# One core, a Fourier transform and two feed-forward layers: the start-up's loads, folds and conversions put in another order

## The chip, the core and the metric

The kernel runs on one core of a Trainium2 chip. The metric is device time in microseconds (us) of one execution; the time before is the median of three runs. Everything else here is read from one execution that was profiled: TensorE (PE) multiplies matrices, PEld is its loading of weights; VectorE (DVE), ScalarE (ACT) and GpSimd (POOL) work elementwise; SyncE (SP) issues the transfers. Each engine works through its own list in order.

## What is computed

```python
X = np.fft.fft(np.fft.fft(x, axis=1), axis=2).real      # x: 2 x 3008 x 256
h = X.reshape(6016, 256) @ moe_w_in                     # 256 x 2048
y = (h * (1 / (1 + np.exp(-h)))) @ moe_w_out            # 2048 x 256
h2 = y @ moe2_w_in                                      # 256 x 2048
out = (np.maximum(h2, 0) + alpha * np.minimum(h2, 0)) @ moe2_w_out
```

## The kernel before

The transform over the 3008 rows is done as 64 x 47. **Stage A** is the 64-point part. For a batch b, x lies in memory in four variants p, s, q, r, cut into four pieces along n (`PIECES`, 4, 4, 2 and 2 wide, 128 columns each). `fold` (line 252) makes p + s and q + r, and from those the sum s and the difference r of the two; `mm` (line 272) multiplies them by the constant `cs[:, FA0:]` into `psa`, copies the result to `ya`, and `store` (line 293) sends rows of it to memory as `ys`. `FOLD0` names the engine of each fold step of batch 0, v for VectorE and p for GpSimd. `load_y` (line 306) fetches the rows back, transposed, as `y`: two loads of 48 partitions for each half h.

**Stage B** (`stage_b`, 47 points) multiplies y by a constant into `psb`, in groups; ScalarE takes the high part z and VectorE the residual. **Stage C** (`stage_c`) makes from z the even part `ce`, the odd part `co` and `cn`; ScalarE copies them to eo (twice) and to n, VectorE makes the residuals of eo. `cc` holds its constants, `ch` and `cl` are their high and low parts.

**The main loop** runs over (chunk, f) steps: six products of eo with `wi` into `pe` and `po`; VectorE makes `t` from n and pe (L568, here t(0), t(1), ... by step), then `hp` and the second t from po; ScalarE takes the silu; `gl` is a residual; and twelve products with `wo` add into `a`, two steps behind (`LAG`).

The weights come as float64 bits. `to_f32` converts 512 columns in five steps: one on ScalarE (L181), two TENSOR_SCALAR (L185, L189) and two SCALAR_TENSOR_TENSOR (L193, L197) on VectorE. `i0` and `i1` are the first two quarters of the first layer's input weights, `o0` and `o1` of its output weights; each has two conversions, and then high and low parts. The results of a conversion stand in `cvi` and `cvo`. `w128` is one row of the weights.

Before round 0 the order is written out by hand in `manual_schedule`: loads of x and constants, stage A of batch 0, then the conversions of i0, w128 and the first half of o0, stage B and stage C of chunk 0, three steps of the second half of o0 (`s1[:EARLY_O0]`). A planner then orders the loop itself; `PLAN` says at which step each other piece of work is offered to it. SP's queue is in the order of the code. `fh` and `fl` are the high and low part of the stage A constant, used by batch 1 alone.

Of the kernel before, what the change touches and what calls it, by code (L numbers as in the profile page):

```python
# [9 lines left out]
F32 = mybir.dt.float32  # L10
F32R = mybir.dt.float32r
U32 = mybir.dt.uint32
# [3 lines left out]
ALU = mybir.AluOpType  # L16
# [27 lines left out]
FOLD0 = "vvvpvvvpvvvvvvvv"  # L44
# [24 lines left out]
def _tables():  # L69
# [19 lines left out]
    row = 4 * (n2 % 12) + 2 * (n2 // 12)  # L89
    for h, (re, im) in enumerate(((co, -si), (si, co))):  # L90
        for j in range(2):
            for to, at in ((R0 + 94 * h, 47 * j), (RS0 + 95 * h, 48 if j else None)):
                if at is None:
                    c[row, to : to + 24] = re[:, :24]
                    c[row + 1, to + 24 : to + 48] = re[:, :24]
                else:
                    c[48 * j + row, to + at : to + at + 47] = re
                    c[48 * j + row + 1, to + at : to + at + 47] = im
# [21 lines left out]
def fft_moe_kernel(  # L120
# [105 lines left out]
    fl = wp.tile([128, 128], F32R, name="fl")  # L226
    slot0 = wp.tile([128, 2, 12], F32, name="slot0")
# [20 lines left out]
    def stage_a(b):  # L248
# [3 lines left out]
        def fold(i):  # L252
            n0, n1 = PIECES[i : i + 2]
            w = 128 * (n1 - n0)
            p, s, q, r = (X[b, i][:, j * w : j * w + w] for j in range(4))
            on = [nc.vector if w == "v" else nc.gpsimd for w in (FOLD1 if b else FOLD0)[4 * i : 4 * i + 4]]
            on[0].tensor_tensor(p, p, s, op=ALU.add)
            on[1].tensor_tensor(q, q, r, op=ALU.add)
# [47 lines left out]
    def load_y(b, h, kh):  # L306
# [3 lines left out]
        src = YS[b, h, kh].rearrange("n (a j k) m -> j (n a) k m", a=4, j=2)  # L310
        for j in range(2):
            last = nc.sync.dma_start(Y[b, kh][48 * j : 48 * j + 48, h, :w, :], src[j])
        return last
# [471 lines left out]
    if True:  # L785
        with tc.manual_schedule():
# [3 lines left out]
            nc.vector.memset(sm, 0.0)  # L790
            nc.scalar.activation(sm[:1, :1], sm[:1, :1], AF.Silu)
            for j in range(len(PIECES) - 1):
                load_x(0, j, (PIECES[j + 1] - PIECES[j]) // 2)
                if j == 0:
                    nc.sync.dma_start(cs[:, :R0], cst[:, :R0])
            cc = conv(F32, "cc")
            for g in range(2):
                load_half("i0", wi1[g], g, 0)
                if g == 0:
                    nc.sync.dma_start(cc, cst[:, CD0:])  # L800
                    nc.sync.dma_start(w128_raw.rearrange("p n t -> p (n t)"), w128.bitcast(U32))
            nc.sync.dma_start(cs[:, R0:], cst[:, R0:CD0])
            fold, mm, rest = stage_a(0)
# [6 lines left out]
            load_half("o0", wo1, 0)  # L810
            for h in range(2):
                load_y(0, h, 0)
            load_half("o0", wo1, 1)
# [3 lines left out]
            run(i00[:4])  # L817
            run(i01[:2])
            run(w128_st[:1])
            nc.scalar.activation(ch, cc, AF.Copy)  # L820
            run(i00[4:])
# [4 lines left out]
            for n, (st, pool) in enumerate(zip(after_i0, SUM0)):  # L826
                (st if callable(st) else st[pool == "v"])()
                if n == 2:
                    run(s0)
            b00, b01 = stage_b(0, 0), stage_b(0, 1)  # L830
            run(b00[:2])
            run(b01[:2])
# [176 lines left out]
```

## Time and profile before

| | |
|---|---|
| runs | 984.6, 981.5 and 984.77 us, median 984.6 |
| the profiled execution's own time | 988.99 us |
| its span | 987.2 us |
| granted TensorE clock over the span | 0.988 |
| busy in the span | PE 957.9 us (97%), DVE 780.8 (79%), ACT 710.7 (72%), POOL 405.4 (41%) |

Times in the rows below count from the span's start. TensorE's share is a mean over stages with different limits: the start-up is the first 60 us or so. A row of the timeline gives the start, the duration of what it merges, the engine, the line, and in brackets how long the engine was idle before it and what ended that.

### The profile page before, as it was taken

The numbers are of one execution on the slowest core, as the hardware profiler recorded it, in microseconds if no ns is written. First come the engines' busy times: TensorE is split into PE (matmuls) and PEld (weight loads), VectorE is DVE, ScalarE is ACT, GpSimd is POOL, SyncE is SP. The second block draws the span as 40 slices with busy tenths as digits, with TensorE's granted clock in tenths as the row PEclk, the third lists the DMA queues.
The fourth block names the chain that finished last, engine by engine and source line by source line (L and its number), as shares of the span: only waits on it lengthen the run. The fifth ranks groups of instructions, "written<-read, shape, count | busy, mean of one in ns | idle before, by whom it ended". The sixth has DMA issues, their size and how long they took to land.

```text
span 987.2 us, 14338 instructions
## 1 busy us (share of the span) xinstructions
PE 957.9 (97%) x5170; PEld 824.7 (84%) x5170; DVE 780.8 (79%) x1328; ACT 710.7 (72%) x1410; POOL 405.4 (41%) x355
## 2 busy tenths in 40 slices
PE   7889899999999999999899999999999999999998
PEld 5768787888878788787789999999999999999997
DVE  6888898676796876958687887878878788787876
ACT  3557566665667666666887888878888788787875
POOL 2677869333257467697641221312213122131200
PEclk9789999999999999999999999999999999999999
DMA  8730300230110201100000000000000000000000
GB/s 264 235 122 3 105 22 1 52 104 1 43 43 9 94 1 43 43 9 35 1 1 22 1 22 22 1 21 1 21 9 14 21 1 21 2 22 21 1 21 21
DMA packets 16614, 37.05 MB, mean 38 GB/s; under 512 B 1824, under 2 KB 11296, under 8 KB 14880
## 3 DMA queue, kind: packets, MB, share of 16 engines
q1 hardware_dynamic: 16544, 36.15, 11.1%
q8 instruction: 40, 0.66, 0.3%
q14 instruction: 30, 0.25, 0.1%
HBM read 26.83 MB, written 9.31 MB: 37 GB/s over the span
## 4 chain that ended last, share of the span: by engine, by line
PE 78%; DVE 9%; issue 5%; POOL 4%; ACT 3%; DMA 1%; SPq 0%; POOLq 0%; ACTq 0%; DVEq 0%
PE a L768 27%; PE ac L670 20%; PE a L610 5%; PE a L612 5%; PE a L608 5%; PE b L670 3%; POOL gl L588 2%; PE po L560 1%; PE po L561 1%; PE pe L560 1%; PE po L562 1%; DVE hp L571 1%; PE pe L562 1%; PE pe L561 1%; PE psb L325 1%
## 5 line engine op out<-in xcount | busy, mean ns | idle before, releaser
L768 PE MATMUL a<-gh,wo 128*128 128x502 f32 x768 | 268.2, 391 | 0.0
L588 POOL TENSOR_TENSOR gl<-t,gh 128x502 fp32r<-128x502 f32 x96 | 131.6, 1371 | 95.1 <-ACT t L576 81.6
L768 PEld LDWEIGHTS a<-gh,wo 128*128 128x128 f32 x768 | 145.0, 189 | 23.2
L737 DVE SCALAR_TENSOR_TENSOR h<-h,fc,q 128x502 f32<-128x502 f32 x192 | 130.3, 679 | 38.4 <-ACT q L732 35.7
L610 PE MATMUL a<-gl,wo 128*128 128x502 f32 x384 | 148.3, 395 | 4.1 <-POOL gl L588 4.1
L768 PE MATMUL a<-gl,wo 128*128 128x502 f32 x384 | 149.7, 391 | 0.0
L612 PE MATMUL a<-gh,wo 128*128 128x502 f32 x384 | 147.3, 393 | 0.0
L748 DVE TENSOR_TENSOR gl<-h,gh 128x502 fp32r<-128x502 f32 x192 | 140.5, 732 | 0.1
L575 ACT ACTIVATE gh<-hp 128x502 fp32r<-128x502 f32 x96 | 59.7, 622 | 92.6 <-DVE hp L571 90.6
L608 PE MATMUL a<-gh,wo 128*128 128x502 f32 x384 | 122.8, 397 | 1.2 <-ACT gh L575 0.8
L743 ACT ACTIVATE gh<-h 128x502 fp32r<-128x502 f32 x192 | 118.5, 617 | 2.1 <-DVE h L737 2.1
L732 ACT ACTIVATE q<-h,fc 128x502 f32<-128x502 f32 x192 | 116.9, 609 | 3.0 <-DVE h L715 1.5
L646 POOL TENSOR_TENSOR xt<-o 128x252 f32<-128x252 f32 x24 | 16.7, 716 | 187.2 <-ACT q L732 131.1
L568 DVE SCALAR_TENSOR_TENSOR t<-n,sm,pe 128x502 f32<-128x502 f32 x96 | 70.2, 731 | 29.0 <-PE pe L562 25.3
L610 PEld LDWEIGHTS a<-gl,wo 128*128 128x128 f32 x384 | 73.2, 191 | 20.7 <-POOL gl L588 5.9
L588 POOL TENSOR_TENSOR gl<-hp,gh 128x502 fp32r<-128x502 f32 x52 | 69.4, 1335 | 47.6 <-ACT hp L576 39.8
L571 DVE TENSOR_TENSOR hp<-t,po 128x502 f32<-128x502 f32 x96 | 64.5, 672 | 29.5 <-PE po L562 23.8
L608 PEld LDWEIGHTS a<-gh,wo 128*128 128x128 f32 x384 | 72.2, 191 | 17.5 <-ACT gh L575 2.2
L612 PEld LDWEIGHTS a<-gh,wo 128*128 128x128 f32 x384 | 73.1, 190 | 15.0
L768 PEld LDWEIGHTS a<-gl,wo 128*128 128x128 f32 x384 | 72.5, 189 | 7.7
L704 ACT ACTIVATE u<-ac 128x252 f32<-128x252 f32 x96 | 36.6, 381 | 51.6 <-PE ac L670 51.6
L656 POOL TENSOR_TENSOR os<-o,os 128x252 fp32r<-128x252 f32 x36 | 32.5, 918 | 94.5 <-ACT os L655 92.6
(191 smaller groups left out, 2296.0 us busy)
## 6 DMA issues: line engine op xcount, KB each, us to landing
out_t<-ot SPq DMA_DIRECT2D x24, 251.0 KB, 2.5
x<-in_xs SPq DMA_DIRECT2D x8, 512.0 KB, 5.6
raw_i<-in_wi SPq DMA_DIRECT2D x8, 512.0 KB, 4.7
raw_w<-in_wi SPq DMA_DIRECT2D x4, 1024.0 KB, 5.0
raw_w<-in_wo SPq DMA_DIRECT2D x4, 1024.0 KB, 4.8
raw_o<-in_wo SPq DMA_DIRECT2D x3, 1024.0 KB, 5.6
y<-ys SPq DMA_DIRECT2D x16, 144.0 KB, 2.9
x<-in_xs SPq DMA_DIRECT2D x2, 1024.0 KB, 4.8
```

Source lines behind the costliest of these rows:

```text
L568: nc.vector.scalar_tensor_tensor(t, E128[c], w128_sb[:, f : f + 1], pe, op0=ALU.mult, op1=ALU.add)
L571: nc.vector.tensor_tensor(hp, t, po, op=ALU.add)
L588: (nc.gpsimd if s or lo_pool(i + 1) else nc.vector).tensor_tensor(lo, h, hi.bitcast(F32), op=ALU.subtract)
L608: nc.tensor.matmul(ACC1[lb, s], hi, G[i, s][0], start=st, stop=False)
L610: nc.tensor.matmul(ACC1[lb, s], hi, G[i, s][1], start=False, stop=False)
L612: nc.tensor.matmul(ACC1[lb, s], lo, G[i, s][0], start=False, stop=sp)
L670: nc.tensor.matmul(to, w, x, start=start and q == 0, stop=q == 2, skip_group_check=True)
L732: nc.scalar.activation(h["q", i][:, to], source(n, part), AF.Abs, scale=coef(n, i, 1))
L737: nc.vector.scalar_tensor_tensor(h[f"h{i}"][:, to], source(n, part), coef(n, i, 0), h["q", i][:, to], op0=ALU.mult, op1=ALU.add)
L743: nc.scalar.activation(hi, H[n][f"h{i}"], AF.Copy)
L748: nc.vector.tensor_tensor(lo, H[n][f"h{i}"], G[n, i][0].bitcast(F32), op=ALU.subtract)
L768: nc.tensor.matmul(ACC2[lb], w[lb][j], x, start=st and first, stop=sp and last)
```

## The change

In batch 0:

- cs, the first constants, is issued from ScalarE, and x is first in SP's queue. raw_i's two halves follow each other, with w128 and cc behind them.
- The first piece's fold stops after p + s and q + r. Its sum and difference are formed in PSUM: two products for each half, the second half's with `fn`, the constant times -1, made on ScalarE. slot0 takes the difference of two columns on GpSimd. The other pieces add p + s and q + r in one operation over two rows of x, and all fold steps of batch 0 are on VectorE.
- Stage B's 96 rows stand in another order, with the constants arranged to fit, so that `load_y` is one load per half; that holds for both batches.
- Both halves of raw_o are loaded behind y. The first half of o0 (`s0`) is converted between stage B's groups and stage C's parts, the three early steps of `s1` stand ahead of n, and fh and fl are made behind chunk 0's n.

```diff
-FOLD0 = "vvvpvvvpvvvvvvvv"
...
-    row = 4 * (n2 % 12) + 2 * (n2 // 12)
+    row = n2 % 12 + 48 * (n2 // 12)
...
+            if first or b:
+                on[0].tensor_tensor(p, p, s, op=ALU.add)
+                on[1].tensor_tensor(q, q, r, op=ALU.add)
+            else:
+                on[0].tensor_tensor(x[:, ::2, :], x[:, ::2, :], x[:, 1::2, :], op=ALU.add)
+            if first:
+                nc.gpsimd.tensor_tensor(slot0[:, b, n0:n1], p[:, ::128], q[:, ::128], op=ALU.subtract)
+                for h, t in ((0, cs[:, FA0 : FA0 + 128]), (1, fn)):
+                    X[b, "f", h, i] = ((cs[:, FA0 : FA0 + 128], p), (t, q))
+                return
...
-        src = YS[b, h, kh].rearrange("n (a j k) m -> j (n a) k m", a=4, j=2)
-        for j in range(2):
-            last = nc.sync.dma_start(Y[b, kh][48 * j : 48 * j + 48, h, :w, :], src[j])
-        return last
+        nc.sync.dma_start(
+            Y[b, kh][:, h, :w, :].rearrange("p k m -> p (k m)"),
+            YS[b, h, kh].rearrange("n (a k) m -> a n (k m)", a=8),
+        )
...
+            nc.scalar.dma_start(cs[:, :R0], cst[:, :R0])
             nc.scalar.activation(sm[:1, :1], sm[:1, :1], AF.Silu)
             for j in range(len(PIECES) - 1):
                 load_x(0, j, (PIECES[j + 1] - PIECES[j]) // 2)
-                if j == 0:
-                    nc.sync.dma_start(cs[:, :R0], cst[:, :R0])
...
+            nc.scalar.activation(fn, cs[:, FA0 : FA0 + 128], AF.Copy, scale=-1.0)
...
-            load_half("o0", wo1, 0)
             for h in range(2):
                 load_y(0, h, 0)
-            load_half("o0", wo1, 1)
+            for i in range(2):
+                load_half("o0", wo1, i)
...
-            run(b00[:2])
-            run(b01[:2])
-            run(p0)
-            run(s1[:EARLY_O0])
-            run(stage_c(0, 0))
+            ev, od, ny = stage_c(0, 0)
+            run(b00[:2] + b01[:1] + s0[:2] + b01[1:2] + s0[2:4] + [ev, s0[4], od] + p0 + s1[:EARLY_O0] + [ny])
...
-        put(*PLAN["fa"], [lambda: split(fh, fl, cs[:, FA0 : FA0 + 128])])
+        put(*PLAN["fa"], [lambda: behind(lambda: split(fh, fl, cs[:, FA0 : FA0 + 128]), 0)])
```

SP's queue from the second constants to the next stores, before (raw_o is o0's bits):

```order
L802 DMA cs<-in_cst 128x378
L295 DMA ys_0_0_129<-ya_0_132 48x10x128
L295 DMA ys_1_0_136<-ya_1_139 48x10x128
L295 DMA ys_0_0_129<-ya_0_132 48x2x128
L295 DMA ys_1_0_136<-ya_1_139 48x2x128
L402 DMA raw_o_190<-in_wo 128x1024
L312 DMA y_0_192<-ys_0_0_129 48x768 x2
L312 DMA y_0_192<-ys_1_0_136 48x768 x2
L402 DMA raw_o_190<-in_wo 128x1024
```

and with the change:

```order
L813 DMA cs<-in_cst 128x378
L308 DMA ys_0_0_129<-ya_0_132 48x10x128
L308 DMA ys_1_0_137<-ya_1_140 48x10x128
L308 DMA ys_0_0_129<-ya_0_132 48x2x128
L308 DMA ys_1_0_137<-ya_1_140 48x2x128
L323 DMA y_0_189<-ys_0_0_129 96x1x768
L323 DMA y_0_189<-ys_1_0_137 96x1x768
L415 DMA raw_o_192<-in_wo 128x1024 x2
```

The first raw_o load has gone from between the stores and y to behind y, and four y loads are two.

ScalarE's list at the end of stage B and in stage C, before:

```order
L343 ACTIVATE z_1_258<-psb_1_3_270 128x63
L450 ACTIVATE wo_0_0_278<-cvo_0_238 128x512
L181 ACTIVATE cvo_1_282<-raw_o_190 128x512
L165 ACTIVATE eo_0_286<-ce_0_287 128x502
L165 ACTIVATE eo_0_286<-co_0_295 128x502
L378 ACTIVATE n_0_301<-cn_0_302 128x502
L450 ACTIVATE wo_0_0_278<-cvo_1_282 128x512
L181 ACTIVATE cvi_0_412<-raw_i_313 128x512
```

and with the change:

```order
L356 ACTIVATE z_1_249<-psb_1_3_264 128x63
L164 ACTIVATE eo_0_274<-ce_0_275 128x502
L164 ACTIVATE eo_0_274<-co_0_284 128x502
L463 ACTIVATE wo_0_0_290<-cvo_0_261 128x512
L180 ACTIVATE cvo_1_294<-raw_o_192 128x512
L391 ACTIVATE n_0_298<-cn_0_299 128x502
L164 ACTIVATE fh<-cs 128x128
L180 ACTIVATE cvi_0_405<-raw_i_308 128x512
```

The high part of o0's first half and the first step of its second half (cvo_1) stood ahead of the two eo copies, and now stand between them and n.

VectorE's list from the last z residuals of stage B to hp of step 0 (t_335 and t_328 are t(0)), before:

```order
L345 TENSOR_TENSOR z_1_258<-psb_1_3_270,z_1_258 128x63
L185 TENSOR_SCALAR cvo_1_282<-cvo_1_282 128x512
L189 TENSOR_SCALAR cvo_1_282<-cvo_1_282 128x512
L166 TENSOR_TENSOR eo_0_286<-ce_0_287,eo_0_286 128x502
L166 TENSOR_TENSOR eo_0_286<-co_0_295,eo_0_286 128x502
L193 SCALAR_TENSOR_TENSOR cvo_1_282<-raw_o_190,cvo_1_282 128x512
L568 SCALAR_TENSOR_TENSOR t_335<-n_0_301,sm,pe_327 128x502
L197 SCALAR_TENSOR_TENSOR cvo_1_282<-raw_o_190,cvo_1_282 128x512
L571 TENSOR_TENSOR hp_337<-t_335,po_328 128x502
```

and with the change:

```order
L188 TENSOR_SCALAR cvo_0_261<-cvo_0_261 128x512
L192 SCALAR_TENSOR_TENSOR cvo_0_261<-raw_o_192,cvo_0_261 128x512
L165 TENSOR_TENSOR eo_0_274<-ce_0_275,eo_0_274 128x502
L196 SCALAR_TENSOR_TENSOR cvo_0_261<-raw_o_192,cvo_0_261 128x512
L165 TENSOR_TENSOR eo_0_274<-co_0_284,eo_0_274 128x502
L184 TENSOR_SCALAR cvo_1_294<-cvo_1_294 128x512
L581 SCALAR_TENSOR_TENSOR t_328<-n_0_298,sm,pe_320 128x502
L188 TENSOR_SCALAR cvo_1_294<-cvo_1_294 128x512
L165 TENSOR_TENSOR fl<-cs,fh 128x128
L584 TENSOR_TENSOR hp_330<-t_328,po_321 128x502
```

o0's first half (cvo_0) stands around the first eo residual, where the second half (cvo_1) stood; of the second half one step is ahead of t(0) and three are behind it, of which one TENSOR_SCALAR and one SCALAR_TENSOR_TENSOR were ahead of it.

## Rows read from the trace of the kernel before

**Rows 1.** Busy us and count of each engine by stretch, then TensorE clock, DMA share, GB/s

```profile
24.80:35.05 10.25, 10.05 (x37) 8.88 (x38) 6.66 (x13) 4.23 (x11) 4.99 (x5) 0.50 0.75 220
35.05:55.50 20.45, 15.92 (x77) 12.01 (x75) 20.35 (x30) 12.42 (x24) 16.18 (x17) 1.00 0.66 220
55.50:62.30 6.80, 5.76 (x14) 4.64 (x15) 4.54 (x10) 3.96 (x8) 6.80 (x5) 0.50 0.38 144
62.40:103.90 41.50, 41.50 (x186) 34.17 (x185) 37.08 (x50) 28.72 (x51) 30.69 (x23) 1.00 0.15 52
...
106.70:110.10 3.40, 3.17 (x8) 2.57 (x9) 3.40 (x6) 0.98 (x3) 0.98 (x2) 0.50 0.00 0
```

**Rows 2.** Timeline of VectorE in stage A: start, us, engine, line, operation, idle before

```profile
4.59 0.69 DVE L257 TENSOR_TENSOR x<-x 128x512 f32<-128x512 f32 x1 [3.42 <-DMA x<-in_xs]
5.84 0.69 DVE L258 TENSOR_TENSOR x<-x 128x512 f32<-128x512 f32 x1 [0.56 <-DMA x<-in_xs]
7.06 0.96 DVE L166 TENSOR_TENSOR fl<-cs,fh 128x128 fp32r<-128x128 f32 x1 [0.53 <-ACT fh L165]
...
9.91 0.69 DVE L258 TENSOR_TENSOR x<-x 128x512 f32<-128x512 f32 x1 [0.58 <-DMA x<-in_xs]
...
14.92 0.42 DVE L260 TENSOR_TENSOR x<-x 128x256 f32<-128x256 f32 x1
```

**Rows 3.** Timeline of SP's queue, stores and y

```profile
14.94 4.06 SPq L295 DMA_DIRECT2D ys<-ya  x4
19.06 0.43 SPq L402 DMA_DIRECT2D raw_o<-in_wo  x1
20.48 1.71 SPq L312 DMA_DIRECT2D y<-ys  x4
```

**Rows 4.** DMA issues over the whole span: count, KB each, median us to landing

```profile
raw_i<-in_wi SPq DMA_DIRECT2D x8, 512.0 KB, 4.7
...
y<-ys SPq DMA_DIRECT2D x16, 144.0 KB, 2.9
```

**Rows 5.** Timeline of TensorE: stage A's first products, stage B's first, pe(4)

```profile
8.68 1.98 PE L281 MATMUL psa<-x,cs 128*128 128x512 f32 x4 [2.24 <-DVE x L259]
...
25.00 3.27 PE L325 MATMUL psb<-cs,y 96*128 96x95 f32 x14 [3.40 <-DMA y<-ys]
...
56.53 0.79 PE L560 MATMUL pe<-eo,wi 128*128 128x502 f32 x1 [2.02 <-DVE t L568]
```

**Rows 6.** Timeline of ScalarE, end of stage B and stage C

```profile
31.81 0.67 ACT L181 ACTIVATE cvo<-raw_o 128x512 f32<-128x512 f32 x1
33.09 0.59 ACT L165 ACTIVATE eo<-ce 128x502 fp32r<-128x502 f32 x1 [0.60 <-PE ce L355]
...
35.18 0.59 ACT L378 ACTIVATE n<-cn 128x502 f32<-128x502 f32 x1 [0.25 <-PE cn L355]
```

**Rows 7.** Timeline of VectorE from o0's first conversion to pe(4)

```profile
25.16 0.69 DVE L193 SCALAR_TENSOR_TENSOR cvo<-raw_o,cvo 128x512 uint32<-128x512 uint32 x1
25.89 1.64 DVE L197 SCALAR_TENSOR_TENSOR cvo<-raw_o,cvo 128x512 uint32<-128x512 uint32 x1
...
33.60 0.43 DVE L189 TENSOR_SCALAR cvo<-cvo 128x512 uint32<-128x512 uint32 x1
33.94 0.68 DVE L166 TENSOR_TENSOR eo<-ce,eo 128x502 fp32r<-128x502 f32 x1
...
36.16 0.73 DVE L568 SCALAR_TENSOR_TENSOR t<-n,sm,pe 128x502 f32<-128x502 f32 x1
...
47.88 1.52 DVE L189 TENSOR_SCALAR cvo<-cvo 128x512 uint32<-128x512 uint32 x1
...
50.72 1.77 DVE L193 SCALAR_TENSOR_TENSOR cvo<-raw_o,cvo 128x512 uint32<-128x512 uint32 x1
...
56.40 0.44 DVE L345 TENSOR_TENSOR z<-psb,z 128x282 fp32r<-128x282 f32 x1
56.76 0.75 DVE L197 SCALAR_TENSOR_TENSOR cvo<-raw_o,cvo 128x512 uint32<-128x512 uint32 x1
```

More of the change, by code (lines that the diff above doesn't have):

```diff
@@ L94, in _tables @@
                     c[row, to : to + 24] = re[:, :24]
-                    c[row + 1, to + 24 : to + 48] = re[:, :24]
+                    c[row + 24, to + 24 : to + 48] = re[:, :24]
                 else:
-                    c[48 * j + row, to + at : to + at + 47] = re
-                    c[48 * j + row + 1, to + at : to + at + 47] = im
+                    c[12 * j + row, to + at : to + at + 47] = re
+                    c[12 * j + row + 24, to + at : to + at + 47] = im
     m = np.arange(128)
@@ L226, in fft_moe_kernel @@
     fl = wp.tile([128, 128], F32R, name="fl")
+    fn = wp.tile([128, 128], F32, name="fn")
     slot0 = wp.tile([128, 2, 12], F32, name="slot0")
@@ L254, in fold @@
             w = 128 * (n1 - n0)
[L255 to L258, printed above, removed]
+            x = X[b, i].rearrange("p (j n) -> p j n", j=4)
+            p, s, q, r = (x[:, j, :] for j in range(4))
+            first = b == 0 and i == 0
+            if b:
+                on = [nc.vector if w == "v" else nc.gpsimd for w in FOLD1[4 * i : 4 * i + 4]]
+            else:
+                on = [nc.vector] * 4
+            if first or b:
+                on[0].tensor_tensor(p, p, s, op=ALU.add)
+                on[1].tensor_tensor(q, q, r, op=ALU.add)
+            else:
+                on[0].tensor_tensor(x[:, ::2, :], x[:, ::2, :], x[:, 1::2, :], op=ALU.add)
[4 more added lines that the diff above has]
+                return
             on[2].tensor_tensor(s, p, q, op=ALU.add)
@@ L798, in fft_moe_kernel @@
                 load_half("i0", wi1[g], g, 0)
-                if g == 0:
-                    nc.sync.dma_start(cc, cst[:, CD0:])
-                    nc.sync.dma_start(w128_raw.rearrange("p n t -> p (n t)"), w128.bitcast(U32))
+            nc.sync.dma_start(w128_raw.rearrange("p n t -> p (n t)"), w128.bitcast(U32))
+            nc.sync.dma_start(cc, cst[:, CD0:])
             nc.sync.dma_start(cs[:, R0:], cst[:, R0:CD0])
+            nc.scalar.activation(fn, cs[:, FA0 : FA0 + 128], AF.Copy, scale=-1.0)
             fold, mm, rest = stage_a(0)
@@ L816, in fft_moe_kernel @@
             w128_st = to_f32(lambda: w128_sb, ("w128", 0, NF), "w128")[1]
-            run(i00[:4])
-            run(i01[:2])
-            run(w128_st[:1])
+            run(i00[:1] + i01[:1] + w128_st[:1])
             nc.scalar.activation(ch, cc, AF.Copy)
-            run(i00[4:])
+            run(i00[1:4] + i01[1:2] + i00[4:])
             for ab in zip(i01[2:], w128_st[1:]):
```

2 lines of the change are left out of this document (removed).

## The prediction

> **What bounds the kernel now.** I read the busy time by stretch first, then the timeline of one engine after another over the first 62 us. The stretch 62.40 to 103.90 has TensorE busy for all of its 41.50 us at the full clock [rows 1]; most of what follows looks like it. No work inside the main loop changes, so the change can move the end by one thing: when TensorE gets into that unbroken stretch, and at which clock. In the timeline it gets there with the first product of the fifth (chunk, f) step, at 56.53, after 2.02 us of waiting for VectorE's t of step 3 [rows 5]. Below I call these pe(4) and t(3).
>
> Two kinds of time lie ahead of it. Up to 25.00 it is loading: x lands, VectorE folds it, the stage A rows go out to memory and come back as y; TensorE waits 3.40 us for y [rows 5]. From 24.80 to 35.05 TensorE is busy for 10.05 of 10.25 us, but at a granted clock of 0.50 (the 1.2 GHz level), and VectorE for 6.66 only. From 35.05 to 55.50 it is the other way round: VectorE is busy for 20.35 of 20.45 us and TensorE for 15.92 [rows 1]. So a gain made before 35 us reaches pe(4) only if VectorE has no more to do between t(0), at 36.16 [rows 7], and t(3).
>
> **Stage A, the x loads.** In the queue, x's first half lands by 4.59, its second by 5.84, and the second half of piece 1 by 9.91 [rows 2]. A 512 KB load thus takes 1.25 us of the queue; the 4.07 us from 5.84 to 9.91 hold two of them and cs, so cs costs 4.07 - 2.50 = 1.57. Issued from ScalarE it still moves the same bytes, beside the first x load. Piece 1 is therefore complete between 0 and 1.57 us earlier; I take 0.7, somewhat under the middle, because the bytes do not go away.
>
> From there VectorE now does everything itself. An add of 512 columns takes 0.69, one of 256 columns 0.42 [rows 2], so 256 more columns cost 0.27 and the new two-row adds take 0.69 + 0.54 = 1.23 (2x512) and 0.69 (2x256), estimates from these rows. From piece 1's landing to the last difference: 1.23 + 2 x 0.69 + 2 x (0.69 + 2 x 0.42) = 5.67. Before it is 14.92 + 0.42 - 9.91 = 5.43, with GpSimd taking one difference. So 0.24 is given back, and stage A ends 0.7 - 0.24 = 0.5 us earlier (bounds -0.2 and 1.3). Taking fl (0.96 at 7.06 [rows 2]) out of piece 0's way buys nothing at the end, since piece 1 waits for its load. Piece 0's two added fp32 products are four passes of about 0.5 (1.98 for four, at 8.68 [rows 5]), 2.0 us of TensorE; they can start when q is done, 5.84 + 0.69 = 6.53, instead of 8.68, so 2.15 us of idle time covers them. Without that cover they would cost the 2.0. The new fn on ScalarE lies in the same idle time.
>
> **From the stores to stage B.** The four stores are issued from 14.94; then raw_o's first half goes out at 19.06, ahead of y at 20.48 [rows 3], and TensorE starts stage B at 25.00, 4.52 us after y's issue. In the change y is right behind the stores, as one 288 KB load per half, and both raw_o halves are behind it. A 144 KB y load takes 2.9 us to land, a 512 KB load 4.7 [rows 4]; between them 288 KB comes to 3.6. That gains 0.9 (bounds 1.6 and -0.2). With stage A's 0.5 stage B starts at 23.6, 1.4 us earlier. SP's queue behind it (the next stores, y, raw_i, alpha) moves forward by about as much: raw_o is only swapped with y.
>
> The y rows tell of loads whose 48 memory rows follow each other at one stride; the new one reads 8 groups of 12 rows, and no row has such a shape. The Trainium skill, "DMA: Bandwidth & Descriptors", section "Why a DMA increments its semaphore by 16 and not by 1", says that a DMA is split over the largest number of engines up to 16 that divides the slowest dimension of both sides, which by it would be 8 here (of 96 and 8) instead of 16 (of 48 and 48). By it the sum would be that of the third rival below, 986.2 to 986.7, and not 985.6.
>
> **Stage B and C.** I take this stretch at the same low clock, since TensorE still idles 2.0 us or more ahead of it (3.40 before, less 1.4). ScalarE's first eo copy then ends at 33.09 + 0.59 - 1.4 = 32.28 [rows 6]. But the order behind the two eo copies is new: o0's high part and the next conversion's first step now stand ahead of n, and the first of them waits for VectorE's last step of that o0 half, which has been put between the two eo residuals. On VectorE the first residual no longer stands behind the conversion step at 33.60, so it runs from 32.28 to 32.96 (0.68 long [rows 7]); the conversion step (0.69, as at 25.16 [rows 7]) ends at 33.65. Then ScalarE: 0.67 + 0.67 + 0.59 [rows 6] gives n at 35.6 and t(0) at 35.65. Of 1.4 us, 0.5 is left at t(0), which was at 36.16 [rows 7].
>
> **What VectorE owes.** The first o0 half (four steps, of which the last two are at 25.16 and, stretched to 1.64, at 25.89 [rows 7]) stood in time in which VectorE waited for y anyway; now it lies in the time before t(0), and so pushes the second half behind t(0): one TENSOR_SCALAR more (0.43) and one SCALAR_TENSOR_TENSOR (0.69), and fl as well (0.29 for 128 columns, by the same 0.27 per 256). That is 1.41. Between t(0) and t(3) two more steps have moved ahead of t(3) that were behind it: a z residual (0.44 at 56.40) and the last o1 step (0.75 at 56.76) [rows 7], 1.19. VectorE has no idle time there to hide any of it [rows 1]. So pe(4) comes 1.41 + 1.19 - 0.5 = 2.1 us later, at 58.6.
>
> Half of that is not lost: before, the clock is 0.50 from 55.50 to 62.30 [rows 1], and pe(4) starts into it. If the low stretch lies where it lay, waiting through 2.1 us of it costs 1.05 us of full-clock work. **The sum is +1.05 us.** Against the profiled execution of 988.99 that is 990.0; the median of the runs is 984.6, 4.4 below the profiled one, so I forecast 985.6.
>
> y loads of the second batch have the new form too; they are issued five loop steps before their use (35 against 40 in PLAN) and are hidden by those. In some places the rest of the program is ordered anew as well, near the second low stretch at 106.70 (3.40 us [rows 1], 1.7 us of work) among others; I price that at zero, with 1.7 us either way in the range.
>
> **The rivals.** *The clock stays up in stage B.* The shorter wait for y may leave TensorE at 2.4 GHz. For it: 10.05 us of work at 0.50 would shrink by 5; against it: 2 us of waiting remain, and the 2.02 us before 56.53 also went with a fall. VectorE's 6.66 us in that stretch stay, so at most 10.25 - 6.66 = 3.6 us reach t(0). pe(4) is then at 55.0. Into the same low stretch that is 1.5 gained, 983.1. If the low stretch behind it vanishes as well, its 2.9 us (half of 5.8) come on top: 980.2.
>
> *The conversions meet GpSimd, and the kernel gets slower.* The same steps took 1.52 at 47.88 and 1.77 at 50.72 [rows 7] where GpSimd was busy. The three steps pushed behind t(0) would cost 1.52 + 1.77 + 0.96 (fl's own row [rows 2]) = 4.25 in place of 1.41. That is 2.84 more: 988.4, and 989.5 if the low stretch moves along and gives nothing back. It decides if GpSimd's o0 and gl residuals begin before these steps are through. Against it: GpSimd is busy for only 4.99 of the 10.25 us before 35.05 [rows 1].
>
> *The one-load y is spread over half as many engines.* It then takes what 576 KB takes, 4.7 or more [rows 4]; stage B starts 1.1 later and so does t(0): 986.2 to 986.7. For it: its memory side is in two strides, which none before is; against it: no row shows a narrow load. The Trainium skill's rule cited above speaks for it.
>
> *cs gains nothing.* The bytes beside x hold it up as before: 0.7 us later, 986.0 to 986.3.
>
> **How the numbers follow.** Forecast 33%, clock up 16% (983.1), clock up and no low stretch later 15% (980.2), conversions against GpSimd 17% (988.4 to 989.5), y on fewer engines 12%, cs gains nothing 7%. The range reaches from 980.0 to 989.0: half of the 980.2 case and a third of the GpSimd case fall outside with the reordering's 1.7, and a little of the rest. A measurement of this kernel can tell about 0.5%, 4.9 us, so 979.7 and 989.5 are the bounds: faster 11% (the 980.2 case with the reordering in its favour), slower 7%, the same 82%.
>
> **What would show it.** Stage A's first store at about 14.4 and stage B's start at 23.6 show the first half; y landing over 4.5 us after its issue shows fewer engines. n at 35.6 and t(0) at 35.65 show the ScalarE chain; pe(4) at 58.6 with VectorE over 99% busy from t(0) shows the debt. A granted clock of 1.00 through stage B, or VectorE idle between t(0) and t(3), would prove me wrong.

## The result: 6.4 us slower in the median

| | before | after |
|---|---|---|
| median of the timed runs, us | 984.7 | 991.07 |
| lowest and highest | 981.5, 985.65 | 990.31, 994.24 |
| the profiled execution's own time | 988.99 | 992.02 |

The ratio is 1.0075, with a 95% interval of 1.0051 to 1.0099: slower. The forecast was 985.6 in a range of 980.0 to 989.0.

The two profiled executions differ by 3.0 us only, the medians by 6.4. Two more profiles of the kernel before, taken unchanged (below), ran 986.80 and 985.62. They agree with the first one up to step 17 within 0.4 us; at t(30) the second copy is 1.6 us ahead, and the first profile loses 2.0 us more behind t(80), where it has a stretch of half clock at 417 to 421 that neither copy has. The second copy is nearest to the median, so I measure against it; the three profiles of the kernel before all ran longer than its median. A second profile of the changed kernel (991.58) agrees with the first within 0.5 us at every step in this table.

Start of VectorE's t of some steps (t(i) as in the prediction), in us, as the timelines give it:

| | t(0) | t(4) | t(10) | t(30) | t(80) | own time |
|---|---|---|---|---|---|---|
| before, first profile | 36.16 | 59.03 | 84.15 | 181.69 | 409.15 | 988.99 |
| before, first copy | 35.78 | 58.64 | 83.85 | 181.47 | 408.90 | 986.80 |
| before, second copy | 35.94 | 58.81 | 83.97 | 180.11 | 407.55 | 985.62 |
| after | 35.24 | 61.30 | 85.05 | 185.03 | 413.88 | 992.02 |
| after, copy | 35.27 | 61.36 | 84.95 | 184.87 | 413.46 | 991.58 |

Against the second copy the changed kernel is 0.7 ahead at t(0), then loses 3.2 to t(4), gains 1.4 to t(10), loses 3.8 to t(30) and 1.4 to t(80), and 0.1 behind it: 6.4 in all. So the changed kernel is 1.1 us behind at t(10), and the other 5.3 us are lost later. From t(10) to t(30) no line of the code was changed; from t(30) on it is the second batch's y loads alone, with the rows that they read.

**The start.** TensorE in the changed kernel (a row has start, duration, engine, line, operation, and in brackets the idle time before it and what ended that; three dots stand for rows left out):

```profile
23.60 1.74 PE L338 MATMUL psb<-cs,y 96*128 96x95 f32 x12 [2.98 <-ACT wi L445]
25.50 0.71 PE L338 MATMUL psb<-cs,y 96*128 96x95 f32 x2 [0.16 <-DMA y<-ys]
...
39.08 0.79 PE L621 MATMUL a<-gh,wo 128*128 128x502 f32 x1 [2.11 <-ACT gh L588]
...
59.07 0.79 PE L573 MATMUL pe<-eo,wi 128*128 128x502 f32 x1 [0.63 <-DVE z L358]
```

Stage B starts at 23.60, where it started at 25.00 [rows 5], but its second half still waits for y at 25.50. (The first wait has ScalarE's wi by name; the first y landed at 23.51, just ahead of its end.) pe(4) is at 59.07 instead of 56.53 [rows 5]. In between there is a gap of 2.11 us in front of the first product with gh. ScalarE shows why:

```profile
34.12 0.58 ACT L391 ACTIVATE n<-cn 128x502 f32<-128x502 f32 x1
34.60 0.30 ACT L164 ACTIVATE fh<-cs 128x128 fp32r<-128x128 f32 x1
37.85 0.66 ACT L180 ACTIVATE cvi<-raw_i 128x512 f32<-128x512 f32 x1 [2.95 <-DMA raw_i<-in_wi]
38.42 0.61 ACT L588 ACTIVATE gh<-hp 128x502 fp32r<-128x502 f32 x1
```

A conversion's first step waits 2.95 us for raw_i, and gh stands behind it. VectorE from there to t(4):

```profile
35.24 0.73 DVE L581 SCALAR_TENSOR_TENSOR t<-n,sm,pe 128x502 f32<-128x502 f32 x1
35.88 0.42 DVE L188 TENSOR_SCALAR cvo<-cvo 128x512 uint32<-128x512 uint32 x1
36.22 0.28 DVE L165 TENSOR_TENSOR fl<-cs,fh 128x128 fp32r<-128x128 f32 x1
...
37.01 0.68 DVE L192 SCALAR_TENSOR_TENSOR cvo<-raw_o,cvo 128x512 uint32<-128x512 uint32 x1
...
41.80 3.20 DVE L192 SCALAR_TENSOR_TENSOR cvi<-raw_i,cvi 128x512 uint32<-128x512 uint32 x2
...
46.95 1.52 DVE L184 TENSOR_SCALAR cvo<-cvo 128x512 f32<-128x512 f32 x1
...
49.64 2.30 DVE L188 TENSOR_SCALAR cvo<-cvo 128x512 uint32<-128x512 uint32 x2
...
52.87 2.44 DVE L192 SCALAR_TENSOR_TENSOR cvo<-raw_o,cvo 128x512 uint32<-128x512 uint32 x2
...
55.82 2.83 DVE L196 SCALAR_TENSOR_TENSOR cvo<-raw_o,cvo 128x512 uint32<-128x512 uint32 x2
...
61.30 0.73 DVE L581 SCALAR_TENSOR_TENSOR t<-n,sm,pe 128x502 f32<-128x502 f32 x1
```

Steps that take 0.42 and 0.68 us alone take up to 1.77 here, where GpSimd is busy too; the longest in the second copy take as long (1.51 and 1.78). The three steps that the change pushed behind t(0) are not among them: 0.42, 0.28 and 0.68.

**By stretch.** Busy time of each engine, first the second copy of before, then the changed kernel:

```profile
core 0: us, PE busy (x) PEld busy (x) DVE busy (x) ACT busy (x) POOL busy (x), PEclk, DMA share, GB/s
22.00:35.00 13.00, 10.21 (x37) 9.04 (x38) 7.81 (x15) 5.86 (x14) 7.26 (x7) 0.61 0.74 215
35.00:59.00 24.00, 18.52 (x83) 14.09 (x83) 23.89 (x38) 15.04 (x30) 19.89 (x19) 0.93 0.69 228
62.30:103.00 40.70, 40.70 (x184) 33.85 (x183) 36.20 (x50) 28.74 (x51) 29.80 (x23) 1.00 0.15 53
110.20:180.00 69.80, 69.80 (x310) 57.45 (x309) 59.06 (x87) 48.33 (x88) 55.58 (x49) 1.00 0.09 31
```

```profile
22.00:35.00 13.00, 11.24 (x46) 9.01 (x47) 6.01 (x14) 6.61 (x15) 5.64 (x7) 0.74 0.78 225
35.00:59.00 24.00, 18.14 (x67) 12.92 (x66) 23.66 (x35) 13.18 (x27) 17.68 (x19) 0.79 0.61 204
62.30:103.00 40.70, 40.70 (x185) 33.86 (x183) 34.21 (x48) 26.31 (x48) 28.19 (x22) 1.00 0.15 53
110.20:180.00 69.80, 66.50 (x291) 53.66 (x291) 58.26 (x85) 46.32 (x83) 54.94 (x49) 1.00 0.09 31
```

Before 35 us VectorE now does 6.01 us of work instead of 7.81; from 35 to 59 it is full in both kernels. TensorE's clock is up for more of the first stretch (0.74 against 0.61), which can account for the earlier t(0); no run shows it by itself. From 110.20 to 180.00 TensorE is busy throughout in the one and idle for 3.30 us in the other, at full clock in both. That last line is what the prediction did not have.

From t(4) to t(10), first in the second copy, then in the changed kernel, TensorE is busy throughout:

```profile
58.81:83.97 25.16, 25.16 (x105) 20.67 (x105) 19.79 (x29) 17.67 (x32) 19.27 (x16) 0.93 0.12 43
61.30:85.05 23.75, 23.75 (x104) 19.67 (x103) 19.35 (x30) 16.84 (x31) 15.97 (x13) 0.98 0.15 52
```

What differs is the clock. A stretch at 0.50 lies at 55.45 to 62.28 in the copy and at 55.53 to 62.35 in the changed kernel, which reaches t(4) later: 3.5 us of it are left behind t(4) in the one, 1.05 in the other. Half of the difference is 1.2 of the 1.4 us gained.

### The profile page after: what moved, and what is told of

Its sections match the earlier page's. It is cut to its first block, busy times and chain, and to the rows that moved or that the text cites. A ratio compares the mean times of both kernels' runs of the same rounds, so it can differ in the third digit from the quotient of the medians.

```text
span 990.2 us, 14321 instructions
## 1 busy us (share of the span) xinstructions
PE 960.6 (97%) x5174; PEld 824.4 (83%) x5174; DVE 777.8 (79%) x1325; ACT 710.9 (72%) x1411; POOL 400.4 (40%) x353
## 4 chain that ended last, share of the span: by engine, by line
PE 80%; DVE 8%; issue 4%; POOL 3%; ACT 3%; DMA 1%; SPq 0%; ACTq 0%; POOLq 0%; DVEq 0%
PE a L781 26%; PE ac L683 20%; PE a L623 6%; PE a L621 6%; PE a L625 6%; PE b L683 3%; PE pe L573 2%; PE pe L575 2%; PE pe L574 1%; POOL gl L601 1%; PE po L573 1%; PE po L575 1%; PE po L574 1%; DVE hp L584 1%; PE psa L294 1%
## 5 line engine op out<-in xcount | busy, mean ns | idle before, releaser
L621 PEld LDWEIGHTS a<-gh,wo 128*128 128x128 f32 x384 | 72.0, 191 | 24.3 <-ACT gh L588 9.0
```

Source lines behind the costliest of these rows:

```text
L621: nc.tensor.matmul(ACC1[lb, s], hi, G[i, s][0], start=st, stop=False)
```

## Experiments

Each gives its median and its ratio to the kernel before in the same series, with the 95% interval. The medians of the kernel before in the four series were 984.3 to 984.6.

### Is it the narrow load of y?

In the trace, the changed load's semaphore gets 8 landings (besides one update 1.1 us after its issue) where each load of the kernel before got 16: it ran on 8 of the 16 DMA engines, 4.0 and 5.0 us from issue to the last landing for 288 KB. Two forms put it on 16. One has other rows, the other the old two loads per half.

```diff
-    row = n2 % 12 + 48 * (n2 // 12)
+    row = 8 * (n2 % 12) + 4 * (n2 // 12)
...
-            YS[b, h, kh].rearrange("n (a k) m -> a n (k m)", a=8),
+            YS[b, h, kh].rearrange("n (a k) m -> (n a) (k m)", a=8),
```

> The changed kernel with one thing different: the rows of y are ordered 8n+a instead of 12a+n, so that the one load per half has 96 rows of one stride as its outer dimension instead of 8 blocks; the tables of stage B follow. Theory 1 (the narrow load): the load on 8 DMA engines (4.0 and 5.0 us for 288 KB) holds up the queue behind it, raw_i lands at 37.8/39.4, ScalarE waits 2.95 us in front of gh(0), and the new stretch at half clock (38.46 to 45.29) follows. Here y should land on 16 engines by 22.5 to 23.5, raw_i by 36.5 to 38, no half-clock stretch at 38.5, and the time should fall by 2 to 5 us against the changed kernel, to 986 to 989. Theory 2 (the conversions moved behind cost VectorE and GpSimd): the landings change, the time stays at 990 to 992, pe(4) stays about 59.

987.33; 1.0033 [1.0020, 1.0046]. y lands on 16 engines, 3.2 and 3.7 us after its issue, and by the median half of the loss is gone. The changed kernel with the two loads per half:

```diff
...
+        for j in range(2):
+            last = nc.sync.dma_start(Y[b, kh][48 * j : 48 * j + 48, h, :w, :], src[j])
```

> The changed kernel with the two transfers per half of the kernel before for y (row order and tables of before); stage A, the raw_o loads behind y, and the conversions as changed. If the 8-engine load is what costs, as the 3.7 us between the changed kernel and its wide form say, this lands by the wide form or 1 us over it: 987 to 989. If what helped in the wide form was the single issue and not the engines: 990 to 992, as the changed kernel.

987.65; 1.0031 [1.0019, 1.0042], as the wide form, so the number of issues is not what counts. But the profile does not show a gain at the start: t(10) comes at 85.20, against 85.05 in the changed kernel. It gains 1.8 us from t(10) to t(30), where all engines have the changed kernel's order, and 1.2 from t(30) to t(80) (more on both below). The narrow load alone, in the kernel before:

```diff
...
-        for j in range(2):
-            last = nc.sync.dma_start(Y[b, kh][48 * j : 48 * j + 48, h, :w, :], src[j])
+            YS[b, h, kh].rearrange("n (a k) m -> a n (k m)", a=8),
```

> The kernel before with only the changed kernel's rows and its one load per half (outer dimension 8). If the narrow load costs by itself, 987 to 990: the second half lands at 26 or later, raw_i 1 us later or more. If it costs only together with the conversions moved behind it, 984 to 986.

986.31; 1.0025 [1.0013, 1.0036]. And the wide one alone, with the first diff's last line in its place:

> The kernel before with only the rows of y ordered 8n+a and loaded with one transfer per half (96 rows as the outer dimension); stage A, queue places of raw_o and conversions as before. Theory: one wide transfer lands some 1 us earlier than two of 48 rows, and nothing else is changed: 982.5 to 984.5, the same or up to 2 us faster than the kernel before. If the load's form does not matter once it is on 16 engines: 984 to 985.

986.12; 1.0016 [1.0004, 1.0028]. Alone, then, the two do not differ, and each is slower than the kernel before, by 1.9 and 1.8 us: the expectation for the wide form was missed, and the narrow one lies between its two. In these kernels raw_o's half is ahead of y; y takes 5.0 and 6.0 us in the narrow form and 4.4 and 6.3 in the wide. Only with the rest of the change is the narrow form the slower one.

My reason for that was raw_i, in front of which ScalarE waits. raw_i first in the queue, in the narrow and in the wide form:

```diff
             rest(1)
+            load_w1(1)
             for h in range(2):
                 load_y(0, h, 1)
-            load_w1(1)
```

> The changed kernel with one move in the queue: raw_i (i1) is issued right behind the two stores of ys_1 and ahead of the two loads of y_1 that wait for them. Theory 1 (the narrow load costs through raw_i, in front of which ScalarE waits with gh(0) behind it): raw_i lands by 33 to 35, the wait of 2.95 us and the PE gap of 2.11 us at 37 are gone, and the 3.7 us between the changed kernel and its wide form go with them: 986.5 to 988.5. Theory 2 (the narrow load costs elsewhere, by y itself or y_1): 990 to 992.

> The wide form (rows 8n+a) with the same move of raw_i ahead of the loads of y_1. In the wide form t(0) comes at 32.3, 3 us ahead of the others, and PE then waits 3.10 us for gh(0) behind raw_i. Theory 1: that gap goes, t(4) comes 1.5 to 3 us earlier, 984 to 986. Theory 2 (VectorE is full from t(0) to t(4), so that what PE no longer waits at 34 it waits later): t(4) within 1 us, 986.5 to 988.

991.24 (1.0069 [1.0054, 1.0084]) and 987.53 (1.0033 [1.0020, 1.0046]): nothing gained in either. ScalarE and VectorE in the narrow form of it:

```profile
36.23 1.23 ACT L180 ACTIVATE cvi<-raw_i 128x512 f32<-128x512 f32 x2
```

```profile
39.65 1.84 DVE L184 TENSOR_SCALAR cvi<-cvi 128x512 f32<-128x512 f32 x2
41.41 1.77 DVE L196 SCALAR_TENSOR_TENSOR cvo<-raw_o,cvo 128x512 uint32<-128x512 uint32 x1
43.10 0.72 DVE L581 SCALAR_TENSOR_TENSOR t<-n,sm,pe 128x502 f32<-128x502 f32 x1
```

The wait for raw_i is gone, but now two conversions run through VectorE in front of t(1), at 43.10 instead of 39.56. The last y landed 1.45 us later in this execution and t(0) is as much later, at 36.69; from t(0) to t(4) it is 26.3 us against 26.1, so the wait that went gave nothing. Theory 1 has fallen: the 2.11 us gap was a symptom. That VectorE's work is short of time instead fits its 23.66 busy us of 24.00. Nor is the narrow load shown to make raw_i late: it landed at 37.8 and 39.4 in the changed kernel, at 38.6 and 39.8 with two loads per half, and in the wide form at 35.9 and 37.9 in one profile, at 38.8 and 40.1 in the other.

A second profile of the wide form told how much of its gain is its own:

> The wide form of the changed kernel, unchanged, profiled once more. In its first profile t(0) came at 32.3, no stretch at half clock lay over t(4), and t(5) was 3.4 us ahead of the changed kernel's. If that is the form's own: t(5) at 63.5 to 64.5 again. If it was chance in the clock: t(4) at 59.5 to 60, t(5) up to 1.9 us later, 65.5 to 66.

990.58, with t(0) at 35.33 and t(4) at 62.79, where the first profile had 32.33 and 59.79. The stretch of stage B and C, first profile and second:

```profile
23.45:33.65 10.20, 9.47 (x48) 6.55 (x47) 7.49 (x17) 5.87 (x14) 4.35 (x6) 1.00 0.75 233
```

```profile
23.45:33.65 10.20, 10.20 (x38) 8.91 (x38) 5.24 (x12) 4.76 (x11) 3.14 (x5) 0.50 0.73 214
```

The granted clock (the third number from the end) was 1.00 in the one and 0.50 in the other, the 2.4 and the 1.2 GHz level, after TensorE's wait in front of stage B of 2.24 and 2.41 us. So the 3 us at t(0) were the clock's, and by chance. The form's runs lie between 986.17 and 991.57. Why the narrow form's median is 3.7 above its median, while the two are alike without the moved conversions, stays open in part: 0.5 us lie between the second profile of the wide form (t(10) at 84.50) and the changed kernel at t(10).

### Is it the conversions?

The kernel before with the order of the conversions, n and fa as changed; queues, stage A and y as before:

```diff
...
-                if n == 2:
-                    run(s0)
...
+            run(b00[:2] + b01[:1] + s0[:2] + b01[1:2] + s0[2:4] + [ev, s0[4], od] + p0 + s1[:EARLY_O0] + [ny])
...
```

> The kernel before with only the conversions reordered (raw_o0's steps between stage B's groups, after_i0 before them, the fa split behind n); queues, stage A and y loads as before. Theory 2: +4 to +6 over the kernel before, 988 to 991. Theory 1: the debt of VectorE alone, +1 to +2, 985.5 to 987. Theory 3 (no part is the loss; a shift of the start moves later stretches on GpSimd and VectorE about by several us either way): no sum, each variant lands somewhere within 4 us.

989.94; 1.0049 [1.0034, 1.0063], the largest of the parts. But this edit changes the loop's order too: its profile is 0.6 us behind the second copy at t(10) (84.54) and 4.2 at t(30) (184.35). t(0) to t(4) takes 25.9 us there (36.72 to 62.62), 26.1 in the changed kernel, 22.9 in the copies of before. Some of its VectorE rows:

```profile
42.04 2.92 DVE L189 TENSOR_SCALAR cvi<-cvi 128x512 uint32<-128x512 uint32 x2
...
47.62 1.55 DVE L197 SCALAR_TENSOR_TENSOR cvi<-raw_i,cvi 128x512 uint32<-128x512 uint32 x1
49.09 0.41 DVE L185 TENSOR_SCALAR cvo<-cvo 128x512 f32<-128x512 f32 x1
49.43 1.74 DVE L197 SCALAR_TENSOR_TENSOR cvi<-raw_i,cvi 128x512 uint32<-128x512 uint32 x1
```

The same without moving the first half of raw_o0; the diff is against that run:

```diff
+                if n == 2:
+                    run(s0)
...
-            run(b00[:2] + b01[:1] + s0[:2] + b01[1:2] + s0[2:4] + [ev, s0[4], od] + p0 + s1[:EARLY_O0] + [ny])
+            run(b00[:2] + b01[:2] + [ev, od] + p0 + s1[:EARLY_O0] + [ny])
```

> The kernel before with the reordered conversions, as in the run with them alone (989.9), but with the first half of raw_o0 still converted where it was, in the time before y lands. Theory (the debt of VectorE: four instructions, 0.43, 0.43, 0.69 and 1.64 us at the old place, are what the reordering puts beside stage B and C): t(0) to t(4) takes 23 us as in the kernel before instead of 25.9, 985 to 987. Rival (ScalarE's order, n behind the conversions, or fa behind n, costs): 988 to 990.

987.62; 1.0034 [1.0021, 1.0047], between the two: by the medians 2.1 of the 5.4 us go with raw_o0's first half, with intervals that overlap, and t(0) to t(4) takes 24.3. In the kernel before that half runs while TensorE waits for y, here in its second copy:

```profile
23.70 0.43 DVE L185 TENSOR_SCALAR cvo<-cvo 128x512 f32<-128x512 f32 x1 [1.25 <-ACT cvo L181]
24.17 0.43 DVE L189 TENSOR_SCALAR cvo<-cvo 128x512 uint32<-128x512 uint32 x1
24.63 0.69 DVE L193 SCALAR_TENSOR_TENSOR cvo<-raw_o,cvo 128x512 uint32<-128x512 uint32 x1
25.35 1.64 DVE L197 SCALAR_TENSOR_TENSOR cvo<-raw_o,cvo 128x512 uint32<-128x512 uint32 x1
```

The other side, VectorE's work taken out: the changed kernel without the last three steps of both halves of raw_o0.

```diff
+            for s in (s0, s1):
...
+                s[2] = s[3] = lambda: None
+                s[4] = lambda box=box: box.__setitem__(0, box[0].bitcast(F32))
```

> The changed kernel without the last three VectorE steps of both halves of raw_o0 (the shift and the two merges), six instructions of 0.42, 0.68 and 0.68 us each, so its output is not the reference's. Theory (from stage C to t(4) VectorE is full, and what the start gains or loses shows there): t(4) comes 2 to 4 us earlier than 61.3. The planner also goes back to the order of the kernel before for GpSimd between 120 and 165 us, so the gaps at 155, 158 and 163 us should be gone and t(30) should lie about 2 us better still: 985 to 987 in all. Rival (PE waits for raw_i and for products anyway): t(4) within 1 us, 989 to 991.

988.85; 1.0041 [1.0023, 1.0059]: 2.2 us under the changed kernel, less than expected. t(4) is at 61.10, as if nothing had been gained, but y and raw_o landed late in the profiled execution (raw_o at 29.9 and 31.2 instead of 27.6 and 28.8) and t(0) was at 36.95; from t(0) to t(4) it is 24.2 instead of 26.1. The loop's order is the old one again from t(10) to t(30), which takes 96.8 instead of 100.0. Since both changed, the median alone tells neither theory apart.

The conversions put back into the old order in the changed kernel, first with raw_o behind y, then with raw_o's first half ahead of a wide y:

```diff
...
+                if n == 2:
+                    run(s0)
...
-            run(b00[:2] + b01[:1] + s0[:2] + b01[1:2] + s0[2:4] + [ev, s0[4], od] + p0 + s1[:EARLY_O0] + [ny])
...
```

```diff
...
+            load_half("o0", wo1, 0)
             for h in range(2):
                 load_y(0, h, 0)
-            for i in range(2):
-                load_half("o0", wo1, i)
+            load_half("o0", wo1, 1)
```

> The changed kernel with the conversions (raw_i0, raw_o0) and the fa split put back in the order of the kernel before; stage A and y as changed. Theory 2 (conversions behind are the loss): 984 to 987, pe(4) back to 56 to 57. Theory 1 (narrow load): raw_i still lands at 37.8/39.4 and gh(0) still waits; 988 to 991.

> Stage A as changed, y on 16 engines with one load per half, but the conversions and raw_o's place in the queue as before. Against the wide form with the conversions moved (987.3) it tells what the moved conversions cost once y is early. Theory (VectorE's debt: the first half of raw_o is converted beside stage B and C instead of in the idle time before it): t(0) is later (33 to 34.5) but t(4) earlier than 59.8, at 57 to 58.5; 984.5 to 986.5. Rival (the moved conversions are free then, the loss over the kernel before is elsewhere): 987 to 988.5.

990.89 (1.0062 [1.0050, 1.0074]) and 988.07 (1.0037 [1.0022, 1.0051]), each in the range of its second theory: neither is clearly faster than the kernel with the conversions moved and the same form of y (991.07 and 987.33). In the first, ScalarE shows the reason:

```profile
27.83 0.66 ACT L180 ACTIVATE cvo<-raw_o 128x512 f32<-128x512 f32 x1 [5.25 <-DMA raw_o<-in_wo]
28.40 0.61 ACT L445 ACTIVATE wi<-cvi 128x512 fp32r<-128x512 f32 x1
28.92 1.04 ACT L356 ACTIVATE z<-psb 128x283 fp32r<-128x283 f32 x4
```

With raw_o behind y, the old order waits 5.25 us for it in front of stage B's evictions: those two edits need each other. In the second, y lands at 25.5 and 26.5, since raw_o's half is ahead of it.

### Is it the order that the planner makes later?

Stage A alone, first (cs on ScalarE's queue, x first, the new folds, in the kernel before):

```diff
+            nc.scalar.dma_start(cs[:, :R0], cst[:, :R0])
...
+            if first:
```

> The kernel before with the stage A part alone: cs through ScalarE's queue, x first, the first piece folded in PSUM, the folds of pieces 2 to 4 as two adds in one. By the prediction's first term the last store goes out 0.5 us earlier and stage B starts 0.3 to 0.9 earlier: 983.5 to 985.5, same as the kernel before within 1 us. If stage A's part itself is the loss (its extra ScalarE pass and the fp32 products), over 987.

985.51; 1.0011 [1.0001, 1.0021]. The first store is at 14.35, against 14.26 and 14.41 in the copies: no gain. This execution had only 3.4 us at half clock in stage B and C (10.2 in the copies), t(0) at 33.33 and t(10) at 79.19, 4.8 us ahead of the second copy. It kept 1.1 of that at t(30), and its timeline has new gaps of 0.7 to 1.1 us at 149, 153 and 157, far from stage A. The joined add alone, in the kernel before, leaves the order of the start as it is but makes the planner order the loop in that other way:

```diff
-            on[0].tensor_tensor(p, p, s, op=ALU.add)
-            on[1].tensor_tensor(q, q, r, op=ALU.add)
...
+                on[0].tensor_tensor(x[:, ::2, :], x[:, ::2, :], x[:, 1::2, :], op=ALU.add)
...
```

> The kernel before with one small thing of the change: the two adds of pieces 2 to 4 joined into one of double width. What runs up to 35 us is then as before within 0.2 us; the planner, though, puts GpSimd's adds in front of gl between 120 and 165 us and ScalarE's steps from 38 us on in the same other order as in the changed kernel. Theory (the planner's order costs by itself): PE gaps of 0.6 to 1.0 us in front of the products with gh and gl at about 128, 155, 158 and 163 us, where the kernel before has none over 0.5, against a shorter gap at 104; +1 to +2.5, 985.5 to 987. Rival (that order is neutral, as the prediction priced it): 984 to 985.

985.55; 1.0013 [1.0000, 1.0025]. What TensorE waited for from 84 to 182 us: first in the first copy of before, then in this kernel, then in the changed one (us in total, times, longest):

```profile
PE po L560 <- DVE t L568: 3.0, 1, 3.0
```

```profile
PE a L612 <- ACT gh L579: 2.3, 2, 1.3
PE a L614 <- POOL gl L592: 1.7, 2, 0.9
```

```profile
PE a L621 <- ACT gh L588: 2.4, 2, 1.4
PE a L623 <- POOL gl L601: 1.7, 2, 0.9
```

The waits are the changed kernel's, and the one of 3.0 us is gone. This profile ran 988.86, the longest of the kernel's twelve runs, so its steps are not those of the median. Its stretch line beside that of the next experiment:

```profile
110.20:180.00 69.80, 66.47 (x288) 53.49 (x287) 58.66 (x83) 46.16 (x84) 52.94 (x48) 1.00 0.07 23
```

From t(4) to t(10) this kernel is 2.1 us faster than the second copy, and 1.6 of that the clock accounts for: its stretch at 0.50 ended at 59.85, 0.2 us behind its t(4). By the medians the net cost of this edit is 1.0 us.

The other way round, the changed kernel with one number of the plan moved, so that the order is the same up to step 12 and other behind it:

```diff
...
-    "c2": (13, 23)
+    "c2": (12, 23)
...
```

> The changed kernel with one number of the plan moved: chunk 2 of stage B and C may begin one step earlier (12 instead of 13). Up to t(12) every engine's order is the changed kernel's; behind it GpSimd's folds and gl stand nearer to the order of the kernel before. Theory (the planner's order from t(13) on costs by itself): the loss of 2.4 us between t(10) and t(30) changes by 1 us or more, 989 to 990.5. Rival (the loss there follows from the lateness at the start and not from the order): t(10) to t(30) as in the changed kernel within 0.5, 991 to 992.

989.50; 1.0054 [1.0032, 1.0076]. In the profile TensorE's idle time in that stretch falls from 3.30 to 0.74 us:

```profile
110.20:180.00 69.80, 69.06 (x300) 55.72 (x299) 59.27 (x86) 49.26 (x89) 56.18 (x49) 1.00 0.08 28
```

t(10) to t(30) takes 96.0 us, as in the second copy (96.1), against 100.0 in the changed kernel. The median is 1.6 lower than the changed kernel's, with intervals that overlap, and the profiled execution, at 986.43, is the shortest of seven that go up to 993.84. It has no stretch at half clock from t(10) to t(30), where the other two have 3.4 us, but that is not the difference: the changed kernel's order takes 34.56 us from t(10) to t(17) with that stretch, and 34.53 in the run with the conversions alone, which has none there.

This one run was not late at t(10) (83.51), so alone it does not part the order from the late start. All the profiles together do. From t(10) to t(30) the engines go through their work in one of three orders:

| order from t(10) to t(30) | profiles | t(10) | t(10) to t(30), us |
|---|---|---|---|
| as before | the kernel before (3), narrow load alone, wide load alone, less VectorE work | 81.98 to 85.94 | 96.1 to 97.6 |
| the changed kernel's, or it but for a few instructions | changed (2) and wide form (2); two loads; raw_i first (2); conversions as before (2); conversions alone (2); stage A alone; joined add alone | 79.19 to 85.51 | 98.1 to 100.0 |
| plan number moved | that one | 83.51 | 96.0 |

```profile
83.97:180.11 96.14, 93.12 (x409) 76.51 (x408) 83.91 (x118) 62.24 (x113) 74.38 (x62) 0.98 0.10 33
85.05:185.03 99.98, 94.62 (x410) 76.44 (x409) 83.84 (x119) 62.83 (x113) 75.78 (x64) 0.98 0.09 32
79.19:179.02 99.83, 94.55 (x410) 76.48 (x409) 84.83 (x118) 62.87 (x113) 75.61 (x64) 0.98 0.10 32
```

These are the second copy, the changed kernel and stage A alone: the last starts 4.8 us ahead of the first and loses as much as the one that starts 1.1 behind it. So the order makes that loss and not the late start. Its size is less sure: the same order takes between 98.1 and 100.0.

From t(30) to t(80) another thing decides, the form of the y loads: the eight profiles with two loads per half take 227.4 to 228.0 us, the seven with the narrow load 228.6 to 229.0, and the five with the wide one 227.3 to 228.4. TensorE does not wait for y there; the planner's order from t(44) to t(60) differs with the form, and from the second copy to the changed kernel 1.2 us lie in that part.

The copies that the table above rests on:

> The kernel before, unchanged, profiled once more. Theory 1 (the profile on which the prediction rested was itself an unlucky one, 4.4 us over its median): here the x pieces land 0.7 to 1.0 us earlier (the last at about 11.65 as in the run with the conversions alone, which has the same queue), the first store is issued at 14.1 to 14.2 instead of 14.94, and t(0) comes before 35.5, with a time of 983 to 985.5. Theory 2 (that profile is typical, and the median of the timed runs differs for reasons late in the span): the last x piece lands at 12.3 to 12.5, the first store is issued at 14.9, t(0) at 36.2.

> The kernel before, unchanged, once more, to see how far two profiled executions of one kernel differ: stretches at half clock begin elsewhere, t(4) within 0.5 us of 58.6 to 59.0, time 982 to 987.

> The changed kernel, unchanged, profiled once more. If what was read in its first profile belongs to the kernel: t(0) within 0.5 us of 35.24, t(4) within 0.5 of 61.3, 2 to 3 us more lost between t(10) and t(30) and 1 to 1.5 between t(44) and t(80) than in the copies of the kernel before. If the wait for raw_i and the stretch at half clock from 38.46 were chance, t(4) is elsewhere by 1 us or more; the losses behind t(10) stay either way, since the order makes them.

In the first copy the last x landed at 11.6 and the first store was issued at 14.26, as the first theory had it, but the time stayed above the median. In the second copy the stretches at half clock up to 110 us lie where they were. The copy of the changed kernel is as the kernel's first profile: 2.3 and 3.8 us more than the copies of before from t(10) to t(30), and 1.1 from t(44) to t(80).

None of the versions is faster than the kernel before.

## Why the prediction was wrong

- **The step that failed: that the change moves the end only by when TensorE gets into the unbroken stretch, with the later order priced at zero (1.7 either way).** Up to t(10) the sum came out, +1.05 forecast and 1.1 measured, and part of that is luck: neither stage A's 0.5 nor y's 0.9 came, yet t(0) was 0.7 earlier (0.5 forecast); the debt was 0.6 larger and 0.4 more was given back. Behind t(10) the changed kernel loses 3.8 us to t(30) against the second copy (2.4 against the first), of which 2.3 (1.7) are idle time of TensorE. The joined add and stage A alone show this loss without the rest of the change, the moved plan number takes it away. Another 1.4 are lost from t(30) to t(80). There the second batch's y loads, said to be hidden by the steps ahead of them, are waited for nowhere, but the order that the planner makes with them is longer: the kernel with the narrow load alone has 1.2 of it. By the medians the parts do not add up this way (the joined add alone is 1.0 slower, the narrow load alone 1.9), and that stays open.
- **VectorE's debt: right mechanism, too small.** 2.6 was forecast from t(0) to t(4), 3.2 measured; pe(4) was put at 58.6 and came at 59.07. The three steps pushed behind t(0) took 0.42, 0.28 and 0.68, which is 1.38 of the 1.41 forecast, so the term that was too small is the 1.19 for the steps that moved ahead of t(3), with 1.8 left for it: its last o1 step, put at 0.75, is one of the two that took 2.83 beside GpSimd. The rival that priced the three steps at 4.25 did not come true, though the time went past its 988.4 to 989.5.
- **Half given back: right, in size and reason.** 1.4 us came back from t(4) to t(10), 1.05 was forecast; the stretch of half clock stayed where it was (55.53 to 62.35), TensorE had no idle time behind t(4), and the later t(4) accounts for 1.2.
- **Stage A 0.5 earlier: wrong.** The 1.57 us for cs was read from an execution in which x landed late: its last piece at 12.4, in the copies at 11.6 and 11.9, in the changed kernel at 11.3. First stores at 14.14 and 14.07 stand against 14.26 and 14.41: 0.1 to 0.3.
- **y 0.9 earlier: wrong.** The estimate of 3.6 us is that of the wide form (3.2 and 3.7). The load ran on 8 engines, as the Trainium skill's rule in "DMA: Bandwidth & Descriptors", "Why a DMA increments its semaphore by 16 and not by 1", has it for these shapes; the trace agrees, with 8 landings. The last y comes at 25.4, and came at 25.3 in both copies. I gave that 12%, and priced it at about 1 us; together with the moved conversions 3.7 us lie between the medians of the two forms. At t(10) the wide form's second profile is 0.5 ahead of the changed kernel, its first, with the clock up, 3.6.
- **ScalarE's chain: right in size.** n ends at 34.12 + 0.58 = 34.70 and t(0) is at 35.24, against 35.6 and 35.65. The clock, which I had taken as low throughout, was up again from 31.63, which can account for n; t(0) then came 0.5 behind n and not 0.05, since the VectorE step ahead of it took 1.05 us at 34.26.
- **The clock stays up in stage B: not in the changed kernel.** It did in the wide form's first profile, with t(0) at 32.3, and brought 986.17: VectorE took up the rest, as the prediction said that it would.
- **SP's queue moves forward: wrong.** raw_i landed at 37.8 and 39.4, 1.5 us later than in the copies. It made the most visible gap, and cost nothing that a run could show; with two loads per half it landed as late, so the narrow loads are not shown to be the reason.

In sum the rivals were all about the start, and of them the narrow load came true. The larger part of the loss lies where the prediction had no mechanism, only an allowance.

## What to carry to other kernels

Where a planner orders the loop from modelled times, compare its output far behind the edit too, and price a changed order by the waits of its own rows, not by zero: here the profiles lose more by it than by the edited part. Work that stands in time in which its engine waits anyway is free only there; before it is moved, look whether that engine is full in the stretch that it moves to. And take a second profile of the kernel before, ahead of reading single landings from the first.

## What was not expected of the hardware

A 288 KB load from memory rows in 8 blocks ran on 8 DMA engines, 4.0 and 5.0 us; with 96 rows as the outer dimension it took 3.2 and 3.7 on 16. Two TENSOR_SCALAR steps of 0.41 us took 2.92 together beside GpSimd (conversions alone, at 42.04). A stretch of 3.4 us at half clock cost nothing from t(10) to t(17): 34.56 us with it (changed kernel) and 34.53 without (conversions alone), in the same order. And two profiles of one kernel can agree within 0.5 us at all steps (the changed kernel) or differ by 3.0 us at t(0) (its wide form, at the two clock levels after waits of 2.24 and 2.41 us).
